# The MLP's hidden units in another order: w4 in runs of seven rows, w3 read at every seventh column

## The chip, the cores and the metric

The kernel runs on one core of a Trainium2 chip. The time is device time in microseconds of one execution. The kernel before took 1092.66 us (median of 3 runs, 1092.45 to 1092.69).

## The reference

Two identical layers run on one token of each of 8 sequences (x is 8 x 1 x 448, everything in bf16). Each layer is attention over a cache, followed by an MLP block:

```python
def _A_ref(x, k_cache, v_cache, wq, wo):        # 16 query heads, 8 key/value heads, 4096 keys, 256 wide
    q = (x @ wq).reshape(B, 1, 16, 256).transpose(0, 2, 1, 3)
    scores = einsum("bhqd,bhkd->bhqk", q, repeat(k_cache, 2)) * (256 ** -0.5)
    o = einsum("bhqk,bhkd->bhqd", softmax(scores), repeat(v_cache, 2))
    return o.transpose(0, 2, 1, 3).reshape(B, 1, 4096) @ wo

def _B_ref(x, w1, w2, w3, w4):                  # w3: 448 x 1792, w4: 1792 x 448
    ...
    x1 = x + hs
    return x1 + _gelu(_layernorm(x1) @ w3) @ w4

x = x + _A_ref(_layernorm(x), ...); x = x + _B_ref(_layernorm(x), ...)   # twice
```

The part `hs` comes from values shifted along a sequence that has only one position, so it is zero: w1 and w2 are never read. What matters here is the last line of `_B_ref`: 1,792 hidden units lie between w3 and w4, and any order of them gives the same sum, provided that the columns of w3 and the rows of w4 are in the same one.

## The kernel before

Nearly all bytes are the caches: 8 sequences x 8 heads x 4096 keys x 256, for keys and for values, and each is read once per layer, apart from some chunks of keys that are kept between the layers. A cache chunk of 128 partitions x 4 KB lands in one of 31 slots in on-chip memory. SyncE (SP) issues the transfers in one fixed order, one, two or four chunks at a time; before each it waits for the last reader of the slots that it reuses. All weights are loaded once, wedged into this stream: wq and wo early, then w3 and w4 in one place (line 1286), and they stay on the chip.

On the compute side a pair of heads goes through these steps. DVE transposes key chunks in 32 x 32 squares (line 960), or PE transposes them and ACT copies them back (lines 878 and 938). PE forms scores (lines 948, 969, 997), DVE, POOL and ACT the softmax, and PE the products with the values (line 1111, and line 1137 with the values as the moving operand). `outproj` multiplies with wo (line 1185).

The layers are interleaved. For each sequence b, `turn(b)` (line 680) comes between its layer 1 and its layer 2: `block` finishes the first layer for one sequence (last part of wo, the norm's sums, the MLP), then the queries of the second layer are formed. The MLP within `block` is, in order:

- `norm1` (line 557): sums over the 448 elements, by four small matmuls with a broadcast stationary operand (line 531), and DVE steps that prepare `syn`.
- `project` (line 580): the product with w3. The hidden units are 14 groups of 128; each group takes four matmuls, three with 128 rows of w3 (line 588) and one with the last 64 rows (line 590), which lie in `w3t_sb`, the first seven groups in its lower 64 partitions and the last seven in its upper 64. So 56 weight loads and 56 matmuls; the stationary operand is 128 x 128 of w3, the moving one is the activation (one column for one sequence).
- `root` (line 535): on DVE meanwhile, the reciprocal root of the variance.
- `gelu` (line 594): DVE line 675 reads the projection's result from PSUM (it waits for the last of the 56 matmuls and for the root), then three more DVE steps with a tanh on ACT in between.
- `down` (line 606): the product with w4, 56 matmuls of line 613, which read `w4_sb[:, k, d0:d0 + 128]` for group k. Line 677 adds the result to x.

`block` runs nine times with one sequence: eight turns, and once more at the very end for the last sequence of the second layer (`end1`). `end` runs the MLP of the second layer for all eight sequences at once (moving operand of eight columns), at about 1052 us.

The order of the instructions on each engine is not written by hand. A planner (`Plan.schedule`) simulates the engines with a cost for each operation and a byte count for each transfer, and writes out one list for each engine; the engines run these lists in order, with semaphore waits. During a turn it holds back long DVE transposes. For w4 the planner is told `P * 12544 * 1.1` bytes.

In `w4_sb` the partition m holds, at place t of 14, row 128 t + m of w4. One row is 448 bf16 values, 896 bytes, and the rows of one partition are not neighbours in memory. The stationary block for group j of `project` is columns 128 j to 128 j + 127 of w3: 128 neighbouring elements in each partition.

Of the kernel before, what the change touches and what calls it, by code (L numbers as in the profile page):

```python
# [3 lines left out]
P = 128  # L4
# [356 lines left out]
def bass_interleave_layers__gqa_block_cached__mixer_s_mlp__decode_kernel(  # L361
# [21 lines left out]
    def sb(name, shape, dt):  # L383
        return nc.alloc_sbuf_tensor(name, shape, dt)
# [7 lines left out]
    w3_sb = sb("w3_sb", [P, 3, F], bf)  # L392
    w3t_sb = sb("w3t_sb", [P, F // 2], bf)
    w4_sb = sb("w4_sb", [P, 14, D], bf)
# [37 lines left out]
    def rows(u, t, ap, nbytes):  # L432

        return plan.load(Unit(u, lambda e, u_: e.dma_start(t, ap), nbytes, slotted=False))  # L434
# [5 lines left out]
    U_w3 = [rows(f"w3{k}", w3_sb[:, k, :], B_w3[k * P:(k + 1) * P, :], P * 3584) for k in range(3)]  # L440
# [6 lines left out]
    wq_rest, w3_rest = ([U_side[i], U_even[i]] for i in range(2))  # L447
    wo_src = A_wo.rearrange("(t m) n -> m t n", m=P)
    U_wo = [rows(f"wo{i}", wo_sb[:, 8 * i:8 * i + 8, :], wo_src[:, 8 * i:8 * i + 8, :], P * 7168 * 1.1) for i in range(4)]
    U_w4 = [rows("w4", w4_sb[:, :, :], B_w4.rearrange("(t m) n -> m t n", m=P), P * 12544 * 1.1)]  # L450

    def chunks(cache, b, h, name, skip=(), most=2):

# [57 lines left out]
    Bs = {k: Buf() for k in ("x1", "x4", "xy", "xw", "yn", "sq", "f", "f1", "xc", "jk", "hf", "ht")}  # L511
# [7 lines left out]
    def dve(emit, cost, reads=(), writes=(), banks=(), name="", **k):  # L519
        return add("dve", emit, max(cost - 75, 50), reads, writes, banks, name=name, **k)  # L520
# [56 lines left out]

        return j // 4 * 4 + j % 2 * 2 + j // 2 % 2

    def project(w, wt, half, j0, j1, rhs, out0, nb, units, bufs, name, place=lambda j: j):  # L580


        def emit(e):
            last = None
            for j in range(j0, j1):
                o = psT[:, out0 + place(j) * nb:out0 + (place(j) + 1) * nb]
                for k in range(3):
                    e.matmul(o, w[:, k, j * P:(j + 1) * P], rhs(0, P, k), start=(k == 0), stop=False)
                i, k = (j, 4) if j < half else (j - half, 3)
                last = e.matmul(o, wt[:, i * P:(i + 1) * P], rhs(0, P, k), start=False, stop=True)  # L590
            return last
        add("pe", emit, (j1 - j0) * 4 * 27, bufs, [], [bT], units, name=name, n=4 * (j1 - j0))

# [60 lines left out]
    def block(b, n, last, base):  # L654


        x = xT[:, :, b]
        dve(lambda e: e.memset(syn, 0.0), 125, [], [Bs["yn"]], name=n + "c0")
        dve(lambda e: e.memset(sx1[64:128, 4:5], 0.0), 125, [], [Bs["x4"]], name=n + "c1")
        dve(lambda e: e.tensor_reduce(sjk[:, :], psT[:, base:base + 24].rearrange("p (s c) -> p c s", c=4), axis=AX.X, op=ALU.add),  # L660
            180, [], [Bs["jk"]], [bT], name=n + "ao")
        dve(lambda e: e.tensor_tensor(sjk[:, :], sjk[:, :], x[:, 0:4], ALU.add), 150, [Bs["jk"], Bx[b]], [Bs["jk"]], name=n + "xa")
        outproj(*last, [0], base)
        dve(lambda e: e.tensor_tensor(sjk[:, :], psT[:, base + 24:base + 28], sjk[:, :], ALU.add), 150, [Bs["jk"]], [Bs["jk"]], [bT], name=n + "xb")
        plan.turn = not base
        outproj(*last, [1], base)
        dve(lambda e: e.tensor_tensor(sx1[:, 0:4], psT[:, base + 28:base + 32], sjk[:, :], ALU.add), 150, [Bs["jk"]], [Bs["x1"]], [bT], name=n + "x1")
        norm1(sx1[:, :], Bs["x1"], Bs["x4"], 40, n + "a")
        rhs = lambda p0, p1, k: syn[p0:p1, k, 1:2]
        project(w3_sb, w3t_sb, 7, 0, 14, rhs, 16, 1, U_w3 + w3_rest, [Bs["yn"]], n + "w3")  # L670
        root(lambda: sf[:, 5:6], lambda k: sf[:, (1, 6, 7, 8)[k]:(2, 7, 8, 9)[k]],
             (WEIGHT[0] / WEIGHT[1], WEIGHT[0] * (EPS[0] - EPS[1]), ALU.mult, ALU.add), [Bs["sq"]], [Bs["f1"]], [], n + "n1", True)
        dve(lambda e: e.scalar_tensor_tensor(sxy[:, :], sxc[:, 0:4], sf[:, 5:6], sx1[:, 0:4], ALU.mult, ALU.add),
            160, [Bs["xc"], Bs["f1"], Bs["x1"]], [Bs["xy"]], name=n + "xy")
        gelu(1, lambda: shf[:, :], lambda: sht[:, :], 16, [], n, 150, lambda e, o, i: e.tensor_single_scalar(o, i, sf[:, 2:3], ALU.mult), Bs["f"])
        down(1, lambda: sht[:, :], 32, [], n + "w4")
        dve(lambda e: e.scalar_tensor_tensor(x[:, 0:4], psT[:, 32:36], 0.5, sxy[:, :], ALU.mult, ALU.add), 150,
            [Bs["xy"]], [Bx[b]], [bT], name=n + "r2")
# [114 lines left out]
    def end():  # L793

        w = Wide(None, wq_sb[:, 0, 0:SLOT])
        u = []
        v3 = lambda a: a.rearrange("p (c b) -> p c b", b=B)
        x1, x3 = w.tile(bf, 40), w.tile(bf, 32)
        b1, by, b3 = Buf(), Buf(), Buf()
        ao, xy = w.tile(f32, 32), w.tile(f32, 32)  # L800
        bao = Buf()
        b1.readers = [r for u_ in U_wq for r in u_.readers]
        dve(lambda e: e.memset(x1()[64:128, 32:40], 0.0), 100, [], [b1], units=u, name="ex0")
        for m in range(HKV // 2):
            outproj8(m, m, plan.prio)
        dve(lambda e: e.tensor_reduce(ao(), psT[:, 0:256].rearrange("p (s c) -> p c s", c=32), axis=AX.X, op=ALU.add),
            450, [], [bao], [bT], units=u, name="eao")
        dve(lambda e: e.tensor_tensor(x1()[:, 0:32], ao(), xT[:, 0:4, :].rearrange("p c b -> p (c b)"), ALU.add), 200, [bao, b1] + Bx, [b1], units=u, name="ex1")
        u_, bu, yn, byn, roots = norm8(w, lambda: v3(x1()), [b1], 320, "e")
        rhs = lambda p0, p1, k: yn()[p0:p1, 8 * k:8 * k + 8]  # L810
        project(w3_sb, w3t_sb, 7, 0, 14, rhs, 32, 8, U_w3 + w3_rest + u, [byn], "ew3")
        mul, br = roots(True, "e")
        mul1, br1 = roots(False, "ey")
        dve(lambda e: mul1(e, xy(), u_()[:, 0:32]), 200, [bu, br1], [by], units=u, name="ey")
        dve(lambda e: e.tensor_tensor(xy(), xy(), x1()[:, 0:32], ALU.add), 200, [by, b1], [by], units=u, name="exy")
        ht, hf = w.tile(bf, 112), w.tile(f32, 112)
        Bg = {k: Buf() for k in ("ht", "hf")}
        gelu(8, hf, ht, 32, u, "e", 280, mul, br, Bg)
        down(8, ht, 160, u, "ew4", Bg)
        dve(lambda e: e.scalar_tensor_tensor(x3(), psT[:, 160:192], 0.5, xy(), ALU.mult, ALU.add), 200, [by], [b3], [bT], units=u, name="er2")  # L820

        def back(e):
            last = None
            for cc in (3, 0, 1, 2):
                d0 = cc * P if cc < 3 else D - P
                o = psT[0:B, 0:224].bitcast(bf)[:, d0:d0 + P]
                last = e.transpose(o, x3()[:, 8 * cc:8 * cc + 8], ident[:, :])
            return last
        add("pe", back, 400, [b3, Bc], [], [bT], u, name="eback")
        xo = w.tile(bf, D)  # L830
        bxo = Buf()
        dve(lambda e: e.tensor_copy(xo()[0:B, :], psT[0:B, 0:224].bitcast(bf)), 450, [], [bxo], [bT], units=u, name="exo")
        late.append(plan.load(Unit("out", lambda e, _: e.dma_start(out[0:B - 1, 0, :], xo()[0:B - 1, :]), 7168, slotted=False),
                              after=bxo.writers))
        return w
# [341 lines left out]
    def outproj(b, m, s, prio, heads=(0, 1), base=0):  # L1177

        for i in heads:
            def emit(e, i=i):  # L1180
                for c in range(4):
                    d0 = c * P if c < 3 else D - P
                    for k in range(4):
                        a = 8 * m + 4 * i + k
                        last = e.matmul(psT[:, base + 4 * (2 * s + i) + c:base + 4 * (2 * s + i) + c + 1], wo_sb[:, a, d0:d0 + P],  # L1185
                                        qo[:, a, b:b + 1] if base else o1[b % 2][:, a:a + 1], start=(k == 0), stop=(k == 3))
                return last
            add("pe", emit, 430, [Bo2[m][i] if base else Bo1[b % 2][m][i]], [], [bT], U_wo, prio=prio, name=f"{'WX'[base > 0]}{b}m{m}{i}", n=16)
# [84 lines left out]
    def others():  # L1273
        keep, plan.prio = plan.prio, -0.7
        Ws.append(end())
        plan.prio = keep
# [3 lines left out]
    k, v = K(0, 0, 2, 2, (0, 0, 1))  # L1280
    weave(k, v[:2])
    weave(K(0, 1, 0), v[2:])
    k, v = K(0, 2, 0, 2, (0, 0, 2))
# [4 lines left out]
    for b in range(B):  # L1288
# [5 lines left out]
        n = b + 1  # L1294
# [24 lines left out]
    for o in seq["sp"]:  # L1319
        u = o.unit  # L1320
# [38 lines left out]
    while made < total:  # L1359
        before = made  # L1360
        for e, q in todo.items():
            while at[e] < len(q):
                o = q[at[e]]
# [93 lines left out]
```

## Time and profile before

| | |
|---|---|
| median of the runs | 1092.66 us |
| the profiled execution | 1093.51 us |
| its span, first to last instruction | 1091.6 us |
| mean granted TensorE clock | 0.603 |
| PE, DVE, ACT, POOL busy | 71%, 76%, 19%, 7% |
| bytes moved by DMA | 448.96 MB, mean 411 GB/s |
| w4: one transfer | 1568 KB, 16.4 us from issue to landing |
| w3: three transfers | 448 KB each, 12.1 us |
| line 588, weight loads (one sequence) | 378, 104 ns each |
| line 613, weight loads (one sequence) | 504, 104 ns each |

How to read it: PE is the matmul itself, PEld the load of its stationary operand; loads overlap with matmuls and with one another, so that the time from one load to the next is shorter than a load. The row of slices cuts the span into 40 equal parts and gives a busy share in tenths. A group `x378` collects instructions of one line and shape. An arrow `A <- B` in the waits says that A stood idle until B. The DMA share of a stretch is the mean busy share of the 16 DMA engines; packets overlap a little, so that it can exceed 1. The time to landing runs from the issue on SP to the last byte's arrival and so contains the queue in front.

### The profile page before, as it was taken

The numbers are of one execution on the slowest core, as the hardware profiler recorded it, in microseconds if no ns is written. First come the engines' busy times: TensorE is split into PE (matmuls) and PEld (weight loads), VectorE is DVE, ScalarE is ACT, GpSimd is POOL, SyncE is SP. The second block draws the span as 40 slices with busy tenths as digits, with TensorE's granted clock in tenths as the row PEclk, the third lists the DMA queues.
The fourth block names the chain that finished last, engine by engine and source line by source line (L and its number), as shares of the span: only waits on it lengthen the run. The fifth ranks groups of instructions, "written<-read, shape, count | busy, mean of one in ns | idle before, by whom it ended". The sixth has DMA issues, their size and how long they took to land.

```text
span 1091.6 us, 33778 instructions
## 1 busy us (share of the span) xinstructions
PE 769.7 (71%) x15440; PEld 522.0 (48%) x15440; DVE 833.1 (76%) x1597; ACT 212.5 (19%) x323; POOL 72.0 (7%) x233
## 2 busy tenths in 40 slices
PE   2466585778576966768667787578766796666877
PEld 2255453465246633565325654365433654446545
DVE  4999559965996499954999569974799839996483
ACT  1022130213011311203112032121221221111300
POOL 0000000000000000000000010000100001000000
PEclk9998566556655655555655565555665555555665
DMA  9999999999999999999999999999999999999995
GB/s 360 406 421 418 410 419 424 422 409 419 428 422 402 415 428 426 423 390 421 427 426 420 392 424 428 426 417 401 425 428 424 412 404 427 425 423 405 401 425 230
DMA packets 54991, 448.96 MB, mean 411 GB/s; under 512 B 5552, under 2 KB 11584, under 8 KB 14656
## 3 DMA queue, kind: packets, MB, share of 16 engines
q1 hardware_dynamic: 54688, 446.42, 98.5%
q8 instruction: 121, 1.98, 0.7%
q10 hardware_dynamic: 160, 0.38, 0.1%
q14 instruction: 22, 0.18, 0.0%
HBM read 446.77 MB, written 0.01 MB: 409 GB/s over the span
## 4 chain that ended last, share of the span: by engine, by line
DMA 34%; DVE 32%; PE 21%; issue 6%; SPq 4%; ACT 2%; POOL 0%; POOLq 0%; DVEq 0%
DVE slots L960 25%; DMA slots<-in_A_k_cache_dram 22%; DMA slots<-in_A_v_cache_dram 12%; PE psV L1137 6%; PE psS L969 4%; SPq L434 3%; DVE pT L1067 2%; PE psV L1111 1%; ACT slots L938 1%; PE psT L702 1%; PE psT L613 1%; PE psS L948 1%; DVE slots L1150 1%; SPq L459 1%; PE psK L878 1%
## 5 line engine op out<-in xcount | busy, mean ns | idle before, releaser
L960 DVE STREAM_TRANSPOSE slots<-slots 128x1024 bf16<-128x1024 bf16 x544 | 647.9, 1228 | 35.5 <-DMA slots<-in_A_k_cache_dram 27.9
L969 PE MATMUL psS<-qe,slots 128*128 128x8 bf16 x5760 | 225.1, 174 | 160.3 <-DVE slots L960 112.8
L969 PEld LDWEIGHTS psS<-qe,slots 128*128 128x128 bf16 x5760 | 190.8, 103 | 249.4 <-DVE slots L960 180.1
L1137 PE MATMUL psV<-slots,pT 128*8 128x512 bf16 x1528 | 186.3, 565 | 21.7 <-DMA slots<-in_A_v_cache_dram 15.9
L938 ACT COPY slots<-psK 128x1024 bf16<-128x1024 bf16 x80 | 78.4, 1015 | 164.3 <-PE psK L878 152.3
L878 PE MATMUL psK<-ident,slots 128*128 128x128 bf16 x640 | 74.7, 303 | 2.7 <-DMA slots<-in_A_k_cache_dram 2.3
L1031 POOL PARTITION_ALL_REDUCE small<-small x64 | 23.8, 372 | 719.8 <-DVE small L1029 466.8
L1148 ACT ACTIVATE slots<-psV 128x512 bf16<-128x512 f32 x48 | 28.7, 597 | 206.8 <-PE psV L1137 206.8
L878 PEld LDWEIGHTS psK<-ident,slots 128*128 128x128 bf16 x640 | 62.4, 140 | 7.5 <-issue 3.9
L997 PE MATMUL psS<-slots,qe 128*8 128x512 bf16 x232 | 56.0, 605 | 9.0 <-DVE slots L960 7.1
L1137 PEld LDWEIGHTS psV<-slots,pT 128*8 128x8 bf16 x1528 | 31.0, 90 | 53.5 <-DMA slots<-in_A_v_cache_dram 20.6
L1111 PE MATMUL psV<-pT,slots 128*128 128x2 bf16 x1568 | 50.7, 165 | 6.6 <-DMA slots<-in_A_v_cache_dram 5.6
L1111 PEld LDWEIGHTS psV<-pT,slots 128*128 128x128 bf16 x1568 | 47.3, 104 | 8.7 <-DMA slots<-in_A_v_cache_dram 6.3
L1067 DVE STREAM_TRANSPOSE pT<-psS 128x128 bf16<-128x128 bf16 x64 | 45.3, 707 | 5.7 <-PE psS L1059 3.0
L1052 ACT ACTIVATE pT<-psS 128x128 bf16<-128x128 f32 x56 | 15.5, 277 | 172.3 <-DVE psS L1049 172.1
L1150 DVE TENSOR_TENSOR slots<-psV,slots 128x512 bf16<-128x512 f32 x48 | 32.5, 676 | 20.5 <-ACT slots L1148 20.4
L1185 PE MATMUL psT<-small,wo_sb 128*128 128x1 bf16 x1024 | 35.1, 166 | 7.3 <-DVE small L1118 5.3
L1159 PE MATMUL psV<-same,slots 128*128 128x4 bf16 x320 | 14.3, 166 | 35.7 <-DVE slots L1150 30.7
L948 PE MATMUL psS<-qo,slots 128*128 128x2 bf16 x768 | 27.9, 167 | 14.8 <-ACT slots L938 10.3
L1185 PEld LDWEIGHTS psT<-small,wo_sb 128*128 128x128 bf16 x1024 | 32.2, 104 | 9.5 <-DVE small L1118 6.6
L638 DVE TENSOR_TENSOR qe<-psT,small 128x32 bf16<-128x32 f32 x32 | 5.9, 184 | 40.2 <-PE psS L969 36.7
L948 PEld LDWEIGHTS psS<-qo,slots 128*128 128x128 bf16 x768 | 24.1, 102 | 22.0 <-ACT slots L938 15.7
(195 smaller groups left out, 744.9 us busy)
## 6 DMA issues: line engine op xcount, KB each, us to landing
slots<-in_A_v_cache_dram SPq DMA_DIRECT2D x149, 1024.0 KB, 9.9
slots<-in_A_v_cache_dram SPq DMA_DIRECT2D x49, 2048.0 KB, 22.8
slots<-in_A_k_cache_dram SPq DMA_DIRECT2D x46, 2048.0 KB, 21.4
slots<-in_A_k_cache_dram SPq DMA_DIRECT2D x67, 1024.0 KB, 14.8
slots<-in_A_v_cache_dram SPq DMA_DIRECT2D x18, 512.0 KB, 8.8
wo_sb<-in_A_wo_dram SPq DMA_DIRECT2D x4, 896.0 KB, 19.2
wq_sb<-in_A_wq_dram SPq DMA_DIRECT2D x3, 1024.0 KB, 10.8
w_sb<-in_B_w_dram SPq DMA_DIRECT2D x1, 1568.0 KB, 16.4
```

The source lines that it names most:

```text
L434: return plan.load(Unit(u, lambda e, u_: e.dma_start(t, ap), nbytes, slotted=False))
L878: last = e.transpose(tile[:, j * P:(j + 1) * P], slots[u.slot][:, o:o + P], ident[:, :])
L938: return e.copy(slots[u.slot][:, 1024 * t:1024 * t + 1024], tile)
L948: last = e.matmul(o, slots[u.slot][:, i:i + P], q, start=(cc == 0), stop=(cc == 1))
L960: return e.transpose(o, i)
L969: last = e.matmul(o, slots[u.slot][:, i:i + P], qe[:, 128 * k + 64 * s + 8 * g:128 * k + 64 * s + 8 * g + 8], start=(g == 0), stop=(g == 7))
L997: last = e.matmul(o, q, K[:, lo:hi + 1:hi - lo, :, g, :], start=(g == 0), stop=(g == 7))
L1067: add("dve", lambda e: e.transpose(pZ[:, :, 0:3:2].rearrange("p n s r -> p n r s"), psS[x][:, 128:192].bitcast(bf).rearrange("p (n r s) -> ...
L1111: last = e.matmul(o, slots[u.slot][:, i:i + P], w, start=(c == 0 and cc == 0 and j == 0), stop=(c == NCH - 1 and cc == 1 and j == 7))
L1137: last = e.matmul(psV[x][32 * i:32 * i + 8, :].rearrange("p (k d) -> p k d", k=2), w, v, start=(s == 0 and c == 0), stop=(s == 1 and c == ...
L1150: add("dve", lambda e: e.tensor_tensor(part(1), psV[x][:, :], part(0), ALU.subtract), 590, [Bhalf[0]], [Bhalf[1]], [bV[x]], [v], prio=at - ...
L1185: last = e.matmul(psT[:, base + 4 * (2 * s + i) + c:base + 4 * (2 * s + i) + c + 1], wo_sb[:, a, d0:d0 + P], qo[:, a, b:b + 1] if base els ...
```

## The change

The hidden units are put in another order. They are cut into two halves of 896. Within a half, partition m holds the seven neighbouring rows 7m to 7m + 6 of w4, so that a partition reads two runs of 6,272 bytes instead of fourteen of 896. Group t of a half then consists of the hidden units t, t + 7, t + 14, ..., and the stationary block that `project` loads for it is every seventh column of w3's half. The halves are those of `w3t_sb`. `project` gets a parameter `step`; with step 1, for wq, it does what it did. The planner's byte count for w4 becomes `P * 12544 * 1.02`. Numbers of instructions, matmul shapes and the addresses that `down` reads stay as they are.

```diff
-    U_w4 = [rows("w4", w4_sb[:, :, :], B_w4.rearrange("(t m) n -> m t n", m=P), P * 12544 * 1.1)]
+    U_w4 = [rows("w4", w4_sb[:, :, :].rearrange("p (h t) n -> p h (t n)", h=2), B_w4.rearrange("(h m t) n -> m h (t n)", h=2, t=7), P * 12544 * 1.02)]
...
-    def project(w, wt, half, j0, j1, rhs, out0, nb, units, bufs, name, place=lambda j: j):
+    def project(w, wt, half, j0, j1, rhs, out0, nb, units, bufs, name, place=lambda j: j, step=1):
...
+                i, k4 = (j, 4) if j < half else (j - half, 3)
+                c0, n = (i * P, P) if step == 1 else (i, half * P - i)
                 for k in range(3):
-                    e.matmul(o, w[:, k, j * P:(j + 1) * P], rhs(0, P, k), start=(k == 0), stop=False)
-                i, k = (j, 4) if j < half else (j - half, 3)
-                last = e.matmul(o, wt[:, i * P:(i + 1) * P], rhs(0, P, k), start=False, stop=True)
+                    e.matmul(o, w[:, k, (j - i) * P + c0:(j - i) * P + c0 + n:step], rhs(0, P, k), start=(k == 0), stop=False)
+                last = e.matmul(o, wt[:, c0:c0 + n:step], rhs(0, P, k4), start=False, stop=True)
...
-        project(w3_sb, w3t_sb, 7, 0, 14, rhs, 16, 1, U_w3 + w3_rest, [Bs["yn"]], n + "w3")
+        project(w3_sb, w3t_sb, 7, 0, 14, rhs, 16, 1, U_w3 + w3_rest, [Bs["yn"]], n + "w3", step=7)
...
-        project(w3_sb, w3t_sb, 7, 0, 14, rhs, 32, 8, U_w3 + w3_rest + u, [byn], "ew3")
+        project(w3_sb, w3t_sb, 7, 0, 14, rhs, 32, 8, U_w3 + w3_rest + u, [byn], "ew3", step=7)
```

## The prediction

> **What bounds the kernel now.** The profiled execution took 1093.51 us: a span of 1091.6 us and 1.9 us around it. The runs shown have a median of 1092.66 us, 0.85 us less; I sum against the profiled execution and add the difference to the median. I read the page's slices first, then the DMA queues, then who waits for whom.
>
> ```profile
> DMA  9999999999999999999999999999999999999995
> GB/s 360 406 421 418 410 419 424 422 409 419 428 422 402 415 428 426 423 390 421 427 426 420 392 424 428 426 417 401 425 428 424 412 404 427 425 423 405 401 425 230
> ...
> q1 hardware_dynamic: 54688, 446.42, 98.5%
> ```
> ```profile
> SPq L459 <- PE psV L1137: 312.4, 96, 8.4
> ```
>
> The DMA engines are busy in all slices but the last: the kernel streams 446 MB, and its time is that stream plus what runs after it. So there are two prices only: microseconds off the stream, and microseconds in which the engines run dry. They can run dry because a transfer needs a free slot, and slots are freed by PE: SP's longest wait, 312.4 us in total over 96 times, is for the value products of line 1137, which stand in PE's queue behind the MLP's steps. The part after the stream is bare, as stretches of time show (columns: stretch, length, busy time of PE, PEld, DVE, ACT, POOL, granted clock, DMA share, GB/s):
>
> ```profile
> 60.00:100.00 40.00, 27.83 (x533) 20.90 (x531) 38.55 (x51) 11.69 (x15) 2.70 (x9) 0.98 1.02 420
> ...
> 116.00:120.00 4.00, 2.79 (x93) 2.66 (x94) 4.00 (x6) 0.00 (x0) 0.00 (x0) 0.50 1.07 380
> ...
> 1083.00:1086.00 3.00, 1.92 (x60) 1.76 (x60) 2.30 (x20) 0.00 (x0) 0.40 (x1) 0.50 0.00 0
> ```
>
> From 1083 us on nothing is transferred and the last sequence's MLP runs alone.
>
> **The w4 transfer.** One transfer of 1,605,632 bytes is cut into 256 runs of 6,272 bytes, not 1,792 of 896. Its bytes pass at 116 to 120 us at 380 GB/s (second row above), where the 8 KB rows of the caches run at 420 (first row): 4.23 us against 3.82, so at most 0.40 us is gained. The other end is nothing. A loss I exclude: the bytes are the same and 256 runs still divide evenly over 16 engines. I take 0.40, since 6,272 bytes are nearest to the 8 KB rows. The stream is the bound from there on, so all of it reaches the end. w4 is first read at 139.68 us, long after it lands, so nothing waits for it. SP issues the same transfers in the same order, and the planner's smaller byte count for w4 moves no instruction on any engine. The second product reads the same 128-column blocks of w4 as before, and the activation between the products works on the same shapes: both cost nothing by themselves.
>
> **The stationary operand.** Ten stages of 56 weight loads (nine single sequences, one batch of eight) now take columns 14 bytes apart; before, 128 neighbours. The timeline shows 56 neighbouring-column loads and, from the norm's sum, four whose column step is zero:
>
> ```profile
> 135.61 0.18 PEld L531 LDWEIGHTS psT<-qe,small 128*128 128x128 bf16 x4 [0.41 <-DVE qe L667]
> ...
> 139.68 1.57 PEld L613 LDWEIGHTS psT<-qe,w_sb 128*128 128x128 bf16 x56 [0.86 <-DVE qe L603]
> ```
> ```profile
> L588 PEld LDWEIGHTS psT<-qe,w_sb x378: 102/104/117, 136.7 to 1085.5; 128*128 128x128 bf16 x189
> ```
>
> One load lasts 104 ns, but they overlap: (1.57 - 0.104) / 55 = 26.7 ns from one to the next, and (0.18 - 0.104) / 3 = 25 ns at step zero. No load in this trace has a step above one, so the price is bounded: below by 26.7 ns (a load can hardly get faster by scattering its columns), above by 104 ns, loads that no longer overlap. Step zero points to the lower end, but it reads one spot. A load of this change walks 1,778 bytes of each partition where one of before walks 256. The trace's clearest scattered access points up: the 128x128 transpose of line 1067 takes 707 ns, 5.5 ns a column, where line 960 takes 1228 ns for 1,024, 1.2 ns each, though part of that is fixed cost. With rows pulling both ways I take the middle, 65 ns: 56 x 38.8 = 2.2 us more in each stage.
>
> [...]
>
> *The last sequence.* Its stage runs uncovered but for the root on DVE:
>
> ```profile
> 1084.05 0.16 PEld L588 LDWEIGHTS psT<-qe,w_sb 128*128 128x128 bf16 x3 [0.63 <-DVE qe L566]
> ```
> ```profile
> 1085.54 0.17 PE L590 MATMUL psT<-qe,w3t_sb 128*128 128x1 bf16 x1
> ```
> ```profile
> 1085.96 0.23 DVE L675 TENSOR_SCALAR qe<-psT,small 128x14 bf16<-128x14 f32 x1
> ```
>
> The stage ends at 1085.71; line 675, which needs it, starts at 1085.96. So 0.25 us is covered and 2.2 - 0.25 = 1.9 us is added to the end. Queued behind 675 on DVE are the steps of the gelu; the second product and the output wait for those.
>
> *The eight turns.* There the same stage ends 0.45 us before line 675 in four turns (248.58 against 249.03 us) and 0.04 us before it in the other four (138.37 against 138.41), in three of which PE pauses for about 0.6 us inside the stage. So the turn is late by 1.7 or 2.1 us. Behind it on PE stand line 1137's products, whose slots SP wants. That is hidden as long as transfers already issued keep the engines fed. I read this cover from issue to landing of 1 MB transfers (the last column, median us), in three stretches: 605 to 618 us, where the engines run slightly dry (383 GB/s over it), 492 to 504, and 618 to 636.
>
> ```profile
> slots<-in_A_v_cache_dram SPq DMA_DIRECT2D x4, 1024.0 KB, 7.5
> ```
> ```profile
> slots<-in_A_v_cache_dram SPq DMA_DIRECT2D x3, 1024.0 KB, 7.5
> ```
> ```profile
> slots<-in_A_v_cache_dram SPq DMA_DIRECT2D x7, 1024.0 KB, 9.5
> ```
>
> 7.5 us is thus the landing time with nothing in front, and what exceeds it is cover. Behind the eight turns the key and value medians average 8.3, 9.7, 8.85, 7.55, 9.4, 9.6, 8.8 and 9.25 us: covers of 0.8, 2.2, 1.35, 0.05, 1.9, 2.1, 1.3 and 1.75. Taken from 2.1 (first, third, fifth, seventh turn) or 1.7, they leave 1.3 + 0 + 0.8 + 1.7 + 0.2 + 0 + 0.8 + 0 = 4.8 us of dry engines. Were the cover gone, it would be 15.
>
> *The batch stage* (1052.3 to 1053.95 us) has PE full around it; its gelu starts only at 1062 us, but behind it on PE the wide scores of line 997 end 1055.9 us and then SP, which waited 9.0 us for them, issues. Those 2 MB transfers land in 10.5 and 14.5 us; dry would be 7.5 + 2.5 (1 MB more at 420 GB/s) = 10.0. Cover 0.5, so 2.2 - 0.5 = 1.7 us.
>
> **Sum:** -0.4 + 1.9 + 4.8 + 1.7 = +8.0 us: 1101.5 for the profiled execution, 1100.7 against the median. At 104 ns (4.3 us a stage) the same subtraction gives 21.4 for the turns, 4.1 and 3.8: +28.9, 1121.6. At 54 ns it gives +4.1, 1096.8.
>
> **Rivals.**
> 1. *The load does not feel the step.* The zero-step row speaks for it, the walk over seven times the bytes against it. Only the transfer's gain is left: 1092.3, no change. It decides below 47 ns a load, where the sum is +2.2 us.
> 2. *Slower loads, but hidden in all turns,* because SP is seldom the one that starves: DMA share is 1.00 or above behind every turn. The fourth turn's landing time speaks against it. Last stage and batch remain: 1.9 + 1.7 - 0.4 = +3.2, 1095.9.
> 3. *Faster:* the stream, 0.4 us ahead, also loses some of its dry moments (DMA share 0.92 at 480 to 485 us and 0.94 behind it, some 2.5 us in all turns). At best -2.9, 1089.8. But those come from waiting for slots, which an earlier w4 doesn't free.
>
> **Chances.** Forecast, visibly slower loads that reach the stream, 0.50; rival 1, 0.33; rival 2, 0.12; rival 3, 0.05. This kernel's measurement tells about 0.2%, 2.2 us, from no change: slower 0.62, same 0.33, faster 0.05. Rivals 1 and 2 and nearly all of the forecast lie between 1092.0 (the gain alone, with 0.3 for noise) and 1121 (loads that don't overlap). The forecast's own range is 1096 to 1121.
>
> **What would show it.** In the trace after, 56 loads of lines 588 and 590 should take 3.6 us, not 1.5; line 675's idle time for them should rise from 0.5 us to about 16; DMA share should dip behind the turns; and 116 to 120 us should pass above 400 GB/s. I am wrong if the loads still come every 27 ns; in size, if the cover differs.

## The result and the profile after

The changed kernel took 1097.3 us (median of 6 runs, 1095.0 to 1099.16), the kernel before in the same series 1092.76 us (6 runs, 1092.45 to 1094.54). The ratio is 1.0037, with a 95% interval of 1.0026 to 1.0048: it is slower, by 2.8 to 5.2 us. The forecast was 1100.7 us, 3.4 us too much and on the right side. The profiled execution has a span of 1095.4 us where the one before had 1091.6.

First the part of it that the prediction rests on, the weight loads. In the changed kernel's code lines 588, 590, 613, 675, 677 and 1137 are 591, 592, 615, 677, 679 and 1139. These are the instructions of the tile that holds w3 and w4, after (min/median/max ns of one, first and last start):

```profile
L615 PEld LDWEIGHTS psT<-qe,w_sb x504: 103/104/118, 140.6 to 1092.4; 128*128 128x128 bf16 x168
L591 PEld LDWEIGHTS psT<-qe,w_sb x378: 131/153/155, 136.2 to 1089.3; 128*128 128x128 bf16 x189
L591 PE MATMUL psT<-qe,w_sb x378: 188/192/215, 136.2 to 1089.4; 128*128 128x1 bf16 x189
```

Line 615 still takes 128 neighbouring columns and still lasts 104 ns; line 591 takes every seventh and lasts 153. The matmul's 165 ns have grown to 192. What counts is the time from one load to the next. The last sequence's stage, after, in the timeline:

```profile
1086.46 0.24 PEld L591 LDWEIGHTS psT<-qe,w_sb 128*128 128x128 bf16 x3 [0.62 <-DVE qe L567]
...
1089.37 0.15 PEld L592 LDWEIGHTS psT<-qe,w3t_sb 128*128 128x128 bf16 x1
1089.42 0.19 PE L592 MATMUL psT<-qe,w3t_sb 128*128 128x1 bf16 x1
1089.72 0.23 DVE L677 TENSOR_SCALAR qe<-psT,small 128x14 bf16<-128x14 f32 x1 [1.27 <-PE psT L592]
```

From the first to the 56th load it is 2.91 us, 52.9 ns a step (before: 26.7), and all ten stages show the same. So the stage takes 56 x 26.2 = 1.47 us more. DVE, which before reached its line 675 after the stage had ended, now sits idle for 1.27 us before the same instruction (now 677), until the stage's last matmul; from the first load to line 677 it is 3.26 us instead of 1.91, so 1.35 us of the 1.47 are added bare.

In three turns, the third, fifth and seventh, less is added. There PE had stopped inside the stage before, for 0.5 to 0.7 us, waiting for nothing that the profile shows:

```profile
622.33 0.10 PEld L590 LDWEIGHTS psT<-qe,w3t_sb 128*128 128x128 bf16 x1 [0.67 <-issue]
```

In the changed kernel these pauses are gone: from the first to the last load these stages went from 2.07, 2.20 and 2.20 us to 2.91, and the time from the first load to line 677 grew by only 0.74 to 0.89 us. In the first turn it grew by 1.48 us and in the other four by 1.09, which is 8.2 us over the eight turns. Over the nine stages of one sequence, the waits for the tile of w3's last rows, before and after:

```profile
  DVE qe L675: 0.5, 2
  DVE qe L677: 10.0, 9
```

That is 10.0 us in nine waits, 1.1 us each, instead of 0.5 us in two. Next the stream, in the page's slices and queues:

```profile
DMA  9999999999999999999999999999999999999995
GB/s 360 406 419 415 419 407 426 423 400 410 428 422 410 409 429 424 422 403 419 425 427 420 387 425 426 427 418 406 425 428 422 409 410 427 426 424 398 414 397 203
DMA packets 53455, 448.96 MB, mean 410 GB/s; under 512 B 5552, under 2 KB 9792, under 8 KB 13120
...
q1 hardware_dynamic: 53152, 446.42, 98.3%
...
w_sb<-in_B_w_dram SPq DMA_DIRECT2D x1, 1568.0 KB, 14.9
```

There are 1,536 packets fewer than before (54,688 to 53,152 on the main queue), which is 1,792 runs less 256, and w4 lands in 14.9 us where it took 16.4. Of the slices, the last two are lower by 28 and 27 GB/s than before (425 and 230); they hold the batch stage and the end. In the others now one kernel is ahead and now the other. What is lost shows as thin places in stretches of 5 us. Columns: stretch, length, busy time of PE, PEld, DVE, ACT, POOL, granted clock, DMA share, GB/s. After:

```profile
116.00:120.00 4.00, 2.80 (x93) 2.66 (x94) 4.00 (x6) 0.00 (x0) 0.00 (x0) 1.00 1.03 425
...
140.00:145.00 5.00, 4.99 (x92) 2.46 (x88) 1.91 (x13) 0.37 (x2) 0.38 (x1) 1.00 0.91 333
245.00:250.00 5.00, 4.75 (x93) 3.75 (x91) 2.65 (x21) 0.00 (x0) 0.40 (x1) 0.50 0.96 333
...
1055.00:1060.00 5.00, 5.00 (x71) 3.12 (x71) 4.64 (x16) 0.51 (x2) 0.96 (x3) 0.50 0.88 364
1060.00:1065.00 5.00, 4.74 (x56) 1.58 (x50) 5.00 (x17) 0.60 (x1) 0.00 (x0) 0.79 0.95 338
```

and the same stretches before:

```profile
140.00:145.00 5.00, 4.99 (x86) 2.32 (x87) 2.04 (x13) 1.11 (x2) 0.38 (x1) 0.50 1.00 395
245.00:250.00 5.00, 4.46 (x92) 2.55 (x92) 3.15 (x26) 0.21 (x1) 0.40 (x1) 0.50 1.00 403
...
1055.00:1060.00 5.00, 4.33 (x53) 1.34 (x44) 4.95 (x19) 1.09 (x3) 0.00 (x0) 0.75 1.02 429
1060.00:1065.00 5.00, 3.67 (x79) 2.21 (x80) 4.29 (x18) 0.30 (x1) 0.12 (x1) 1.00 1.00 419
```

w4's bytes pass at 425 GB/s (before 380). Behind the first two turns and behind the batch stage the stream thins out. And SP's longest wait has grown, from 312.4 us in 96 waits to

```profile
SPq L460 <- PE psV L1139: 323.0, 100, 8.4
```

which fits transfers that are issued later because the value products, queued behind the slower stage on PE, free their slots later. It is a hint and no more: the second-longest wait, for the scores of line 971 (969 before), fell from 210.7 to 197.2 us, and all of SP's waits together rose from 797.5 to 815.3.

One pair of traces cannot carry the account further: 24 executions of the kernel before on one chip spread from 1091.5 to 1096.4 us, as much as the whole effect. The experiments therefore rest on ratios over several rounds, and on stretches that several kernels show alike.

### The profile page after: what moved, and what is told of

Its sections match the earlier page's. It is cut to its first block, busy times and chain, and to the rows that moved or that the text cites. A ratio compares the mean times of both kernels' runs of the same rounds, so it can differ in the third digit from the quotient of the medians.

```text
span 1095.4 us, 33778 instructions
## 1 busy us (share of the span) xinstructions
PE 780.2 (71%) x15440; PEld 536.9 (49%) x15440; DVE 833.9 (76%) x1597; ACT 212.2 (19%) x323; POOL 72.2 (7%) x233
## 3 DMA queue, kind: packets, MB, share of 16 engines
q1 hardware_dynamic: 53152, 446.42, 98.3%
## 4 chain that ended last, share of the span: by engine, by line
DVE 33%; PE 27%; DMA 26%; issue 5%; ACT 4%; SPq 4%; POOL 0%; DVEq 0%
DVE slots L962 26%; DMA slots<-in_A_k_cache_dram 21%; PE psV L1139 7%; PE psS L971 6%; DMA slots<-in_A_v_cache_dram 5%; SPq L434 3%; PE psT L591 2%; DVE pT L1069 2%; PE psV L1113 2%; PE psS L950 2%; ACT slots L940 1%; PE psT L615 1%; ACT slots L1244 1%; DVE slots L1152 1%; PE psT L1187 1%
## 5 line engine op out<-in xcount | busy, mean ns | idle before, releaser
L1161 PEld LDWEIGHTS psV<-same,slots 128*128 128x128 bf16 x320 | 11.8, 103 | 46.6 <-issue 38.7
## 6 DMA issues: line engine op xcount, KB each, us to landing
w_sb<-in_B_w_dram SPq DMA_DIRECT2D x1, 1568.0 KB, 14.9
```

## The experiments

What was open after the result: whether the transfer or the operand costs the time, where it is lost (turns, batch stage, last stage), what sets the pace of a load, and whether the runs of w4 can be had without the price.

### One half at a time

The new w4 transfer alone, w3 read as before:

```diff
-        project(w3_sb, w3t_sb, 7, 0, 14, rhs, 16, 1, U_w3 + w3_rest, [Bs["yn"]], n + "w3", step=7)
+        project(w3_sb, w3t_sb, 7, 0, 14, rhs, 16, 1, U_w3 + w3_rest, [Bs["yn"]], n + "w3", step=1)
...
-        project(w3_sb, w3t_sb, 7, 0, 14, rhs, 32, 8, U_w3 + w3_rest + u, [byn], "ew3", step=7)
+        project(w3_sb, w3t_sb, 7, 0, 14, rhs, 32, 8, U_w3 + w3_rest + u, [byn], "ew3", step=1)
```

> The new load of w4, with w3 read at neighbouring columns in all ten stages (so the hidden units of the two products no longer match, and the output is another). Theory A, the strided weight loads cost and the longer runs of w4 gain: 0.4 us less than before, about 1092.4, not to be told from before; 116 to 122 us pass at about 420 GB/s, loads 27 ns apart. Rival B, the earlier w4 shifts the stream against the slots and itself costs time: 1095 to 1097.

Measured: 1092.72 us (11 runs), ratio 0.9996 (0.9987 to 1.0005). The transfer is faster in the stretch, though its whole gain is too small to be told from nothing as a time:

```profile
116.00:120.00 4.00, 2.23 (x73) 2.09 (x74) 4.00 (x6) 0.00 (x0) 0.00 (x0) 0.73 1.01 419
```

The operand alone, w4 loaded as before:

```diff
-    U_w4 = [rows("w4", w4_sb[:, :, :].rearrange("p (h t) n -> p h (t n)", h=2), B_w4.rearrange("(h m t) n -> m h (t n)", h=2, t=7), P * 12544 * 1.02)]
+    U_w4 = [rows("w4", w4_sb[:, :, :], B_w4.rearrange("(t m) n -> m t n", m=P), P * 12544 * 1.1)]
```

> The old load of w4, with every seventh column of w3 as in the changed kernel (output another, the units don't match). Theory A: all of the loss and none of the gain, 4.6 us over before, about 1097.4; the 56 loads take 3.0 us a stage. Rival B: as before, 1092.8, since the loads hide behind the root and the slots.

Measured: 1098.76 us (5 runs), ratio 1.0055 (1.0042 to 1.0069). Its stretches at w4 and behind the batch stage:

```profile
116.00:120.00 4.00, 2.86 (x101) 2.69 (x99) 4.00 (x6) 0.00 (x0) 0.00 (x0) 0.50 1.07 383
1060.00:1065.00 5.00, 5.00 (x52) 1.56 (x46) 5.00 (x13) 0.66 (x2) 0.00 (x0) 0.57 0.80 275
```

383 GB/s against 419 and 425: the rate follows the length of the runs, not the operand. The operand alone makes the kernel slower, and the transfer gives back a few tenths of a microsecond that no interval here can separate from nothing.

### What a load's pace depends on

Other steps in the eight turns, one for each. In the first kernel the steps are 1 to 7 and 1:

```diff
-                c0, n = (i * P, P) if step == 1 else (i, half * P - i)
+                c0, n = (i * P, P) if step == 1 else (i, (P - 1) * abs(step) + 1)
...
-        project(w3_sb, w3t_sb, 7, 0, 14, rhs, 16, 1, U_w3 + w3_rest, [Bs["yn"]], n + "w3", step=7)
+        project(w3_sb, w3t_sb, 7, 0, 14, rhs, 16, 1, U_w3 + w3_rest, [Bs["yn"]], n + "w3", step=7 if base else (1, 2, 3, 4, 5, 6, 7, 1)[b])
```

> One step for each turn: 1, 2, 3, 4, 5, 6, 7, 1 in the eight turns, 7 in the batch and in the last stage (the output is another). [...]

In the second they are 7 to 14, and all four loads of a group read the part of w3 with 128 rows, so that its last 64 rows are left out:

```diff
-                c0, n = (i * P, P) if step == 1 else (i, half * P - i)
-                for k in range(3):
-                    e.matmul(o, w[:, k, (j - i) * P + c0:(j - i) * P + c0 + n:step], rhs(0, P, k), start=(k == 0), stop=False)
-                last = e.matmul(o, wt[:, c0:c0 + n:step], rhs(0, P, k4), start=False, stop=True)
+                c0, n = (i * P, P) if step == 1 else (j, (P - 1) * step + 1)
+                for k in range(4):
+                    if step == 1:
+                        s = w[:, k, j * P:j * P + P] if k < 3 else wt[:, c0:c0 + n]
+                    else:
+                        s = w[:, k % 3, c0:c0 + n:step]
+                    last = e.matmul(o, s, rhs(0, P, k if k < 3 else k4), start=(k == 0), stop=(k == 3))
...
+        project(..., n + "w3", step=1 if base else (7, 8, 9, 10, 11, 12, 13, 14)[b])
...
+        project(..., "ew3", step=1)
```

> Steps 7, 8, 9, 10, 11, 12, 13, 14 in the eight turns, 1 in the batch and the last stage; all four loads of a group are from the 128-row part of w3, so the last 64 rows are left out there (the output is another). [...] Step 7 here should give 53 as in the changed kernel.

Measured (one execution each, 1093.93 and 1094.74 us), as the time from one load to the next:

| step of columns | 1, 2, 3 | 4 | 5 | 6 | 7 | 8 | 9 to 14 |
|---|---|---|---|---|---|---|---|
| ns from load to load | 27 | 33 | 40 | 47 | 53 | 60 | 57 to 60 |

How such a number is read, for step 4 in the first of the two kernels, first and last load of the stage:

```profile
488.70 0.18 PEld L591 LDWEIGHTS psT<-qe,w_sb 128*128 128x128 bf16 x3 [0.45 <-DVE qe L567]
...
490.52 0.12 PEld L592 LDWEIGHTS psT<-qe,w3t_sb 128*128 128x128 bf16 x1
```

(490.52 - 488.70) / 55 = 33.1 ns. The stages of step 3 and 5 contain a pause of 0.5 and 0.2 us, which is left out. And for steps 8 and 14 in the second, where all 56 loads are one line:

```profile
247.31 3.45 PEld L595 LDWEIGHTS psT<-qe,w_sb 128*128 128x128 bf16 x56 [0.44 <-DVE small L569]
...
1014.69 3.44 PEld L595 LDWEIGHTS psT<-qe,w_sb 128*128 128x128 bf16 x56 [0.57 <-DVE qe L567]
```

3.45 us less one load of 0.17, by 55: 60 ns, and the same for 14. So the price begins above step 3, rises by 6.6 ns a step up to 8, and is flat from there. The bytes that a load walks do not set the pace alone: from step 8 to step 14 they grow from 2,032 to 3,556 in each partition, and it stays at 57 to 60 ns. What gives it this shape no run here shows. All this is at a granted clock of 0.5 (for step 7 in the second kernel, in the first turn, the profile gives 1.00; the last section shows why such a figure there is not to be trusted).

### One stage at a time

Each of the three places was put back to neighbouring columns, beside the changed kernel itself on the same chip. The changed kernel once more:

> The changed kernel once more, beside the next three on the same chip: 4 to 5 us over before, about 1097.

```diff
-        project(w3_sb, w3t_sb, 7, 0, 14, rhs, 16, 1, U_w3 + w3_rest, [Bs["yn"]], n + "w3", step=7)
+        project(w3_sb, w3t_sb, 7, 0, 14, rhs, 16, 1, U_w3 + w3_rest, [Bs["yn"]], n + "w3", step=1 if base else 7)
```

(the last stage alone)

> The changed kernel with neighbouring columns in the last sequence's stage alone (its units don't match there). Theory A, the last stage is bare and each part adds up: 1.4 us less than the changed kernel, about 1095.8. Rival B, what counts is the stream: no change, 1097.

```diff
-        project(w3_sb, w3t_sb, 7, 0, 14, rhs, 32, 8, U_w3 + w3_rest + u, [byn], "ew3", step=7)
+        project(w3_sb, w3t_sb, 7, 0, 14, rhs, 32, 8, U_w3 + w3_rest + u, [byn], "ew3", step=1)
```

(the batch stage alone)

> The changed kernel with neighbouring columns in the batch stage alone (its units don't match there). Theory A, read from when each byte arrived in the two traces, where the stream falls behind by 1.8 us at 1050 to 1065 us: 1.8 us less than the changed kernel, about 1095.4. Rival B, the batch hides: no change, 1097.

```diff
-        project(w3_sb, w3t_sb, 7, 0, 14, rhs, 16, 1, U_w3 + w3_rest, [Bs["yn"]], n + "w3", step=7)
+        project(w3_sb, w3t_sb, 7, 0, 14, rhs, 16, 1, U_w3 + w3_rest, [Bs["yn"]], n + "w3", step=7 if base else 1)
```

(the eight turns)

> The changed kernel with neighbouring columns in the eight turns alone, strided in the batch and the last stage (units don't match in the turns). Theory A, the turns' lag is taken back by dry moments that then don't come: 0 to 0.5 us less than the changed kernel, about 1096.8. Rival B, the turns carry the loss as the prediction had it (2.2 of its 4.1 us at 54 ns): 2 us less, about 1095.

And, in a later series, the seventh column in the eight turns only:

```diff
+        project(..., n + "w3", step=1 if base else 7)
...
+        project(..., "ew3", step=1)
```

> The new load of w4, every seventh column in the eight turns alone, neighbouring columns in the batch and the last stage (units don't match there). Theory A, the turns reach the stream as the prediction's covers have it (2.2 us at 54 ns): 1.8 us over before with the transfer's 0.4 taken off, about 1095. Rival B, dry moments take the lag back: as w4_only, 1092.7.

| columns seven apart in | us (runs) | ratio to before |
|---|---|---|
| all ten stages, again | 1098.16 (5) | 1.0046 (1.0030 to 1.0062) |
| all but the last | 1096.27 (8) | 1.0026 (1.0012 to 1.0040) |
| all but the batch | 1095.5 (11) | 1.0021 (1.0012 to 1.0029) |
| last and batch | 1094.82 (11) | 1.0013 (1.0004 to 1.0022) |
| the eight turns | 1095.3 (8) | 1.0027 (1.0015 to 1.0039) |

One theory fell here. After the first pair of traces, comparing when the same bytes had arrived, I believed that what a turn loses is taken back before the end, since the two streams stood level again at 1017 us. The eight turns by themselves cost 1.0027 x 1092.6 - 1092.6 = 2.9 us (1.6 to 4.3), and without them 1.4 us (0.4 to 2.4) are left. Both kernels contain w4's gain of 0.4 us; 2.9 + 1.4 + 0.4 = 4.7 us, against 5.0 for all stages in the repeat. The parts add up within their intervals, and the turns carry rather more than half. Single removals (2.2, 2.7 and 3.6 us, each by about two) are too wide to say more.

The stretch from 1055 to 1065 us, behind the batch stage, says something more. Mean GB/s of its two halves, one execution of each kernel:

| kernel | columns in the batch stage | GB/s | bytes late, us |
|---|---|---|---|
| before | neighbouring | 429, 419 | 0 |
| all but the batch | neighbouring | 423, 424 | 0 |
| the eight turns only | neighbouring | 415, 421 | 0.1 |
| runs of three rows (below) | three apart | 415, 418 | 0.2 |
| steps 7 to 14 | neighbouring | 397, 408 | 0.5 |
| new w4 transfer alone | neighbouring | 388, 398 | 0.7 |
| steps 1 to 7 | seven apart | 392, 428 | 0.3 |
| last and batch | seven apart | 397, 370 | 1.0 |
| changed kernel again | seven apart | 408, 349 | 1.1 |
| all but the last | seven apart | 395, 316 | 1.6 |
| changed kernel | seven apart | 364, 338 | 1.7 |
| operand alone | seven apart | 392, 275 | 2.2 |

The last column is (848 - sum of the two) x 5 us / 420. The dip is deeper with a strided batch stage, 1.3 us on average against 0.3 in the others, so that this stage is worth about 1.0 us. The two groups overlap, so one pair of executions would not have shown it. The first two turns show the same way: from 136 to 260 us five kernels with columns up to three apart there pass 416 to 419 GB/s, seven with columns seven or eight apart 409 to 414; 5 of 417 GB/s over 124 us is 1.5 us. The remaining six turns cannot be seen one by one: their stretches differ as much between kernels with equal turns.

### Is it PE's time, whatever the reason?

If only the lateness of the stage counts, slower matmuls with plain loads must cost the same. The first attempt issued all 56 matmuls twice in the kernel before:

```diff
-                for k in range(3):
-                    e.matmul(o, w[:, k, j * P:(j + 1) * P], rhs(0, P, k), start=(k == 0), stop=False)
-                i, k = (j, 4) if j < half else (j - half, 3)
-                last = e.matmul(o, wt[:, i * P:(i + 1) * P], rhs(0, P, k), start=False, stop=True)
+                i, k4 = (j, 4) if j < half else (j - half, 3)
+                for _ in range(2 if name.endswith("w3") else 1):
+                    for k in range(3):
+                        e.matmul(o, w[:, k, j * P:(j + 1) * P], rhs(0, P, k), start=(k == 0), stop=False)
+                    last = e.matmul(o, wt[:, i * P:(i + 1) * P], rhs(0, P, k4), start=False, stop=True)
```

> The kernel before (old w4, neighbouring columns), with all 56 loads and matmuls of the product with w3 issued twice, the second time over the first: 112 loads 27 ns apart, so that PE is held as long as by 56 strided ones. Theory A, all that counts is the time on PE: as stride_only, 1098 to 1099. Rival B, the strided reads disturb other readers of the on-chip memory as well: less, 1095 to 1096.

Measured: 1108.5 us (4 runs), ratio 1.0139 (1.0124 to 1.0153), three times the loss of the operand's kernels. It decides nothing, because it brought a cost of its own. From the idle times before the instructions of the tile with w3 and w4 (what ended them, us, times), in the kernel before and in this one:

```profile
  issue: 3.6, 7
  issue: 18.6, 14
```

"issue" is time in which PE waited for nothing that the profile shows; before it was 3.6 us in 7 pauses, here 18.6 in 14. Those 15 us are nearly as much as the whole loss of 16. Doubling a stage by its instructions is no test of a stage that is slower with the same instructions. What the pauses are the trace doesn't name, and no run tries it. They are of the kind that three turns of the kernel before have. In kernels with neighbouring columns some of the eight turns have one of 0.4 us or more inside this stage (before three, last and batch two, new w4 transfer alone one); among the 48 strided turns of six kernels there is one, of 0.2 us.

The second attempt keeps the number of instructions: the kernel before, with neighbouring columns, and a moving operand repeated to 64 columns.

```diff
+                r = rhs
+                if name.endswith("w3"):
+                    o = psT[:, out0 + j * nb:out0 + j * nb + 64].rearrange("p (r b) -> p r b", b=nb)
+                    r = lambda p0, p1, k: rhs(p0, p1, k).unsqueeze(1).to_broadcast([P, 64 // nb, nb])
...
+                    e.matmul(o, w[:, k, j * P:(j + 1) * P], r(0, P, k), start=(k == 0), stop=False)
...
+                last = e.matmul(o, wt[:, i * P:(i + 1) * P], r(0, P, k), start=False, stop=True)
```

> The kernel before (old w4, neighbouring columns, the same number of instructions), with the moving operand of the product with w3 repeated to 64 columns in all ten stages; a group's 63 further columns are overwritten by the next group, and only the first is used. At the granted clock of 0.5 a matmul of 64 columns should hold PE about as long as a strided load, 53 ns. Theory A, all that counts is the time on PE: as stride_only, 1098 to 1099. Rival B, the strided reads of the on-chip memory disturb other engines' reads beside their own length: 1095 to 1096 here, with the same time from one matmul to the next.

Measured: 1098.63 us (5 runs), ratio 1.0055 (1.0041 to 1.0068), the same as with the operand alone. Loads and matmuls of this kernel:

```profile
L592 PEld LDWEIGHTS psT<-qe,w_sb x378: 97/107/117, 136.7 to 1093.3; 128*128 128x128 bf16 x189
L592 PE MATMUL psT<-qe,w_sb x378: 216/220/239, 136.7 to 1093.3; 128*128 128x64 bf16 x189
```

The loads are nearly as short as before (107 ns against 104), the matmuls 220 ns instead of 165, and a stage of one sequence advances by 56.5 ns a matmul (the last one, at a granted clock of 0.50), 55 x 29.8 = 1.64 us longer than before. (The batch stage is 1.0 us longer: its matmuls start from 1059.2 to 1061.7 us, where before it was 1052.3 to 1053.8. The granted clock was 0.50 from 1055 to 1060 us and 0.88 from 1060 to 1065.) So a stage that is about 1.5 us longer costs this kernel some 6 us in its ten places (4.5 to 7.5 by the two intervals), whether it is the loads or the matmuls that take the time. Rival B's 1095 to 1096 us lies below the interval (1097.4 to 1100.3). If strided reads disturb other readers besides, it is by less than these intervals can show.

### Runs of three rows

From the table of steps, a step of 3 should be free. Three neighbouring rows of w4 on a partition give runs of 2,688 bytes; 12 of the 14 groups then take every third column of a block of 384, and the seventh group of each half stays as it was:

```diff
+    w4h, w4s = w4_sb[:, :, :].rearrange("p (h q) n -> p h q n", h=2), B_w4.rearrange("(h r) n -> h r n", h=2)
+    U_w4 = [rows(f"w4{b}", w4h[:, :, 3 * b:3 * b + 3, :].rearrange("p h t n -> p h (t n)"),
+                 w4s[:, 384 * b:384 * b + 384, :].rearrange("h (m t) n -> m h (t n)", t=3), P * 5376 * 1.03) for b in range(2)]
+    U_w4 += [rows("w42", w4h[:, :, 6, :], w4s[:, 768:896, :].rearrange("h m n -> m h n"), P * 1792 * 1.1)]
...
+                s = 1 if step == 1 or i == 6 else step
+                c0, n = (i * P, P) if s == 1 else (384 * (i // 3) + i % 3, 127 * 3 + 1)
...
```

> Runs of three rows instead of seven: each half is two blocks of 384 rows and one of 128, so that the columns of w3 are three apart (12 of 14 groups) or neighbours (2 of 14), and w4 comes as 512 runs of 2,688 bytes and 256 of 896, in three transfers. Theory A, steps up to three cost nothing: loads 27 ns apart, and the time of before less a part of the 0.4 us, 1092.4 to 1092.8. Rival B, any scattered column costs: 1095 or more.

Measured: 1092.41 us (11 runs), ratio 1.0000 (0.9992 to 1.0009). The loads and the stretch of w4:

```profile
L595 PEld LDWEIGHTS psT<-qe,w_sb x378: 103/106/118, 136.2 to 1083.8; 128*128 128x128 bf16 x189
```
```profile
116.00:120.00 4.00, 2.91 (x103) 2.83 (x104) 4.00 (x6) 0.00 (x0) 0.00 (x0) 0.50 1.04 409
```

106 ns a load, 27.6 ns from load to load, 409 GB/s. The price of the operand is gone and most of the rate is kept, 4 to 5 us better than the change, but it can't be told from the kernel before: w4 is loaded once, and a few tenths of a microsecond are all there is to gain.

## Why the prediction was right, and where it was off

- *Direction and mechanism: right.* The loads feel the step, the stage on PE gets longer, the stream behind it thins out (with slots that come free later as the reason that SP's waits suggest); and the last stage is bare. Loads at the old pace (rival 1) fell with 52.9 ns; turns that hide it (rival 2) fell with 1.0027 for the turns alone; a faster kernel (rival 3) fell with 1.0037.
- *The mis-sized term: the time from load to load.* I took 65 ns, the middle between 27 and 104; it is 52.9. So a stage is longer by 1.47 us and not by 2.2, and as every later term is this number less a cover, each came out too large. The middle was taken for want of a row with a step between 1 and many; the range held both ends.
- *Luck in the sum at 54 ns.* The text's own subtraction there gave +4.1 us, 1096.8 against the 1097.3 measured. That it comes so near is luck in part: in the turns it counts both the lateness and the cover too high, as the next points show.
- *w4's transfer: right as a rate* (425 GB/s at 116 to 120 us, forecast above 400, worth 0.4 us), though as a time only 0.9996 (0.9987 to 1.0005).
- *Last stage: right in kind.* Forecast 1.9 us; with the true pace the same subtraction, 1.47 less the cover of 0.25, gives 1.2, and 1.35 was measured. The cover was 0.12 and not 0.25: line 675 started 0.42 us after the start of the last matmul, and line 677, which does wait for it, starts 0.30 us after, not when the modelled end of it is drawn.
- *Eight turns: too late and too well covered.* Forecast 4.8 us; with 1.47 us a stage the covers leave 1.8, and less w4's gain 1.4, where the turns alone measured 2.9 (1.6 to 4.3). The text let the whole added time fall on the three turns in which PE paused; the pauses went, and these turns are late by 0.74 to 0.89 us. With the lateness of the trace its covers leave 1.7 us, 0.7 of it in the first two turns, where the stream lost about 1.5. So more came through than the covers allow, at least there. That each turn has the cover that I gave it is not shown.
- *Batch stage: as the cover has it.* Forecast 1.7 us; with 1.47 us a stage it would be 1.0, and the dips behind it are worth about 1.0 on average.
- *Signs named beforehand:* 56 loads take 3.06 us (2.91 + 0.15; forecast 3.6); line 677 waits 10.0 us (forecast about 16); the stretch of w4 is above 400 GB/s; the DMA share dips behind the first two turns and the batch.

The terms as measured, -0.4 + 1.35 + 2.9 + 0.4 + 1.0 = 5.3 us (the 0.4 since the 2.9 already contain w4's gain), stand against 4.0 and 5.0 in the two series of the changed kernel. They agree within their intervals, no better.

## What to carry to other kernels

What a layout gains in a transfer has to be set against every read of the tile and of its partner: here a gain of 0.4 us in one transfer stood against 0.7 to 1.5 us in each of ten stages. Before giving a stationary operand a column step, measure the time from one load to the next at that step: in bf16 columns up to 3 apart cost next to nothing here (27.6 ns against 26.7), 7 apart doubled it (52.9 ns), at a granted clock of 0.5. And where a stage stands in front of the instructions that free the stream's buffers, read the slack from issue to landing: of the 8.2 us by which line 677 was later in the turns, 3.3 reached the end (2.0 to 4.7).

## What the runs showed beyond the expectation

- The price of the step is measured at half clock, and whether it holds at the full clock stays open. The first turn's stage of the changed kernel looks like the exception, since the profile gives a granted clock of 1.00 there and the loads come every 53 ns all the same:

```profile
136.00:139.20 3.20, 3.00 (x56) 3.03 (x56) 1.35 (x14) 0.00 (x0) 0.40 (x1) 1.00 1.03 428
```

But PE does not run at it. The 12 products of 512 columns right behind the stage take 1.45 us, as long as the same 12 in the kernel before (first line), where the clock was 0.50; at 175 us, where it is 1.00 and PE does run faster, 16 of them take 1.04 us:

```profile
138.30 1.45 PE L1137 MATMUL psV<-slots,pT 128*8 128x512 bf16 x12
139.25 1.45 PE L1139 MATMUL psV<-slots,pT 128*8 128x512 bf16 x12
175.01 1.04 PE L1139 MATMUL psV<-slots,pT 128*8 128x512 bf16 x16
```

- Loads of neighbouring columns hardly gain from the full clock: 56 loads of line 615 at 1065.93 us, at a granted clock of 1.00, take 1.47 us, (1.47 - 0.095) / 55 = 25.0 ns from one to the next, against 26.7 at 0.5. Right behind them eight products of 512 columns take 0.60 us, where eight took 1.07 at 145 us, so that PE does run faster there.
- A step of 3 is nearly as fast as a step of 1 (27.6 ns against 26.7), and no step up to 14 costs more than 60 ns: the loads keep overlapping, and the upper bound of 104 ns is never reached.
- 560 more matmuls brought 15 us of pauses on PE that the profile puts down to nothing but issue, up to 2.35 us in one place.
- Single executions of one and the same kernel differ by up to 6.5 us (all but the last, 1093.2 to 1099.7). Reading from one pair of traces that the turns' loss is taken back was an error that only the ratio over several rounds showed.
